# One step's carried state and decay scans, moved ahead of a total and a gated layer on VectorE

## The chip, the cores and the metric

The kernel runs on one core of a Trainium2 chip. A core has five engines, each with its own queue, in which instructions are issued strictly in the order of the program: TensorE (PE in the profile; PEld are its weight loads), VectorE (DVE), ScalarE (ACT), GpSimd (POOL) and SyncE (SP), which here only issues transfers. An engine waits for another one by a semaphore, and whatever stands behind the waiting instruction on its queue waits too. The metric is device time in microseconds, the median of several executions. The profile is of one execution.

## The reference

Two blocks run one behind the other. The first is a state-space scan over 4 batches of 8 heads, 768 tokens long, with heads of 32 columns and a state of 16:

```python
for c in range(nc):                                   # chunks of the sequence
    cum = np.cumsum(la, axis=-1)                      # la = log(clip(a))
    L = np.exp(cum[..., :, None] - cum[..., None, :]) * causal
    M = np.einsum('bhin,bhjn->bhij', Cc, Bc) * L
    y_intra = np.einsum('bhij,bhjd->bhid', M, xc)
    y_inter = np.einsum('bhin,bhnd->bhid', Cc, state) * np.exp(cum)[..., None]
    y[:, :, sl] = y_intra + y_inter
    state = decay_full * state + np.sum(Bx, axis=2)   # carried to the next chunk
```

The second takes the result as 3072 tokens of 256 columns through four experts with 1024 hidden columns each:

```python
for e in range(E):
    h = np.maximum(x @ w1[e], 0.0)
    out += p[:, e:e + 1] * (h @ w2[e])
```

All of it is in float32.

## The kernel before

The scan works in chunks of 128 tokens, 24 in all. Chunks 4k to 4k+3 form block k: one chunk of each of the four batches, at the same place k of the sequence, 512 tokens together. Six blocks follow each other. While the second half of the computation (the experts) works on block k, the scan of block k+1 is done in between.

The experts of a block take eight steps, one for each expert and half of its hidden columns. So n runs over 48 steps, `k, r = divmod(n, 8)`, and r is the step within the block. Steps 0 and 1 are done plainly ahead of the loop; from n = 2 on a step forms its two 2x2 block products from seven products each, with sums in place of the eighth:

- first layer, `fmul(n, 1..7)`: two matmuls each (four records in the profile), gathered in two banks of PSUM called X and Y. `snap` (ScalarE, line 530) copies X aside; `total` (VectorE, line 535) adds a snap to Y; `gated` (VectorE, line 545) applies the maximum with zero and the gate and writes the hidden layer `h`. There are four of these in a step: 11, 22, 21, 12.
- second layer, `smul(n - 1, 1..7)`, one step later: it takes the h's and their four differences T1 to T4 (`diff`, VectorE, line 552), and gathers in four other banks (line 608). T3 and T1 are made at the end of step n, T2 and T4 early in step n+1, from the list `late`.

A bank is written again only when all reads of it are done. Thus `fmul(n, 3)`, which adds into Y, waits for the total of 22, which reads Y as it was before.

Within the steps of block k lies the scan for block k+1, whose chunks are 4k+4 to 4k+7:

- at r = 0, 2, 4, 5 (`scanned`): the decay matrix LT of one chunk, in two halves (VectorE, line 364, `decay_part` 0 and 1), and a small product on GpSimd (line 369);
- at r = 3 and 6 (`scored`), for two chunks together: `masks` (ScalarE), `decay_part(c, 2)`, which is a scan over the decays of one chunk on VectorE (line 347, tile `dec`, from `ah`, which a transfer brings) and a product with it on GpSimd (line 350, tile `cts`); then `scores` (TensorE, line 393, tile `g`), eight matmuls of 32 rows into two banks of their own and into Y and X, and `masked` (VectorE, line 405), the product with LT, eight instructions;
- at r = 4 and 7 (`done`): `outputs` of two chunks (TensorE, lines 450 and 462);
- `carry(c)`, the state that is carried from chunk to chunk (VectorE: a transpose, line 486; for later blocks a multiply-add, line 488; and the masked copy M, line 493). One of these hangs at the end of `late`, behind T2 and T4, in the steps that have one.

The four `scores` of each chunk go to banks `att`, `att`, Y and X. Those on Y wait for the total of 12 and those on X for the gated 21, which free the banks; `masked` waits for all of them.

The order of the work is written out by hand in the loop over n (lines 818 to 919). Nothing is moved by a scheduler. A step that has `scored` issues on VectorE: total and gated 11; the list `late`; total and gated 22; total 12; gated 21; `masked`; gated 12; T3; T1. The variable `behind` is true for r = 3 and r = 6 of block 0, that is n = 3 and n = 6; there the state and the decay scans stand behind gated 21, and in the other blocks they stand ahead of total 12.

GpSimd, in the first eight steps alone, also makes the sums S1 to S4 of the weights (`sum_w1`, `sum_w2`, lines 189 to 193, four instructions for each tile) and stores them to memory for the other blocks (lines 201 and 207). In n = 3 it has the two products of line 350 first, and the sums of w1 of step 5 and w2 of step 4 behind them. SyncE's order of loads in n = 3 is the weights of step 5 and then chunk 7 (tokens and decays).

Of the kernel before, what the change touches and what calls it, by code (L numbers as in the profile page):

```python
# [17 lines left out]
def kernel(  # L18
# [129 lines left out]
    def load_chunk(c):  # L148
        load_tokens(c)
        load_decays(c)  # L150
        load_heads(c)
# [3 lines left out]
    def load_w1(n):  # L155
        e, jj = divmod(n % SPB, JJ)
        t1 = wt1[n] = wts.tile([P, 7, HB], FP32, tag="wt1", name="wt1", bufs=5)
        for k in range(2):
            w = 2 - 2 * k
            a_ = 2 if n < SPB or k else 1  # L160
            nc.sync.dma_start(
                out=t1[:, w:w + a_],
                in_=w1[e, k * P:k * P + P].rearrange("p (a f) -> p a f", a=2)[
                    :, 0:a_, jj * HB:jj * HB + HB])
        if n >= SPB:
            nc.sync.dma_start(out=t1[:, S3:], in_=w1_d[n % SPB])

    def load_w2(n):
        e, jj = divmod(n % SPB, JJ)
        t2 = wt2[n] = wts.tile([P, 7 * HB], FP32, tag="wt2", name="wt2", bufs=5)  # L170
        for i in range(2) if n < SPB else (1,):
            f = i * FH + jj * HB
            nc.sync.dma_start(
                out=t2[:, (1 - i) * 2 * HB:(2 - i) * 2 * HB].rearrange("p (j m) -> p j m", j=JJ),
                in_=w2[e, f:f + HB].rearrange("(j p) m -> p j m", p=P))
        if n >= SPB:
            nc.sync.dma_start(out=t2[:, 2 * HB:], in_=w2_d[n % SPB])
# [137 lines left out]
    def load_gate(k, e):  # L315
        g = gate[k, e] = ffn.tile([P, CPB, P], FP32, tag="gate", name="gate", bufs=3)
        nc.sync.dma_start(out=g, in_=p_d.rearrange(
            "(i k) e s -> k e i s", k=NBLK)[k, e].partition_broadcast(P))
# [54 lines left out]
    def masks(c):  # L373

        s = st[c]
        m = s["ctm"] = att.tile([HN, NT, P], FP32, tag="ctm", name="ctm")
        for t in range(NT):
            nc.scalar.mul(m[:, t], s["xb"][:, OCT:OCT + P], tmask[:, t:t + 1])
# [148 lines left out]
    def snap(n, i):  # L527

        s = first[n][i] = ffn.tile([P, JJ, HB], FP32, tag="snap", name="snap", bufs=4)
        nc.scalar.copy(out=s, in_=first[n]["X"])  # L530

    def total(n, i, b):

        z = first[n]["z" + b] = ffn.tile([P, JJ, HB], FP32, tag="z", name="z", bufs=3)
        nc.vector.tensor_add(z, first[n]["Y"], first[n][i])  # L535

    def gated(n, b, src):

        if n not in hid:
            hid[n] = {}  # L540
        h = hid[n][b] = ffn.tile([P, JJ, HB], FP32, tag="h" + b, name="h" + b)
        k, e = n // SPB, n % SPB // JJ
        half = int(b[1]) - 1
        g = gate[k, e].rearrange("p c s -> p (c s)")[:, half * HB:half * HB + HB]
        nc.vector.scalar_tensor_tensor(  # L545
            out=h, in0=first[n][src], scalar=0.0, in1=g.unsqueeze(1).to_broadcast([P, JJ, HB]),
            op0=ALU.max, op1=ALU.mult)
# [67 lines left out]
    def keep(k, u):  # L615
        e = kept[k, u] = ffn.tile([P, 2, HB], FP32, tag=f"kept{u}", name=f"kept{u}", bufs=1)
        nc.scalar.copy(out=e, in_=acc[k, u])

    def combine(k, part):

        p1, p3 = kept[k, 0][:, 0], kept[k, 0][:, 1]
        if part == 0:
            kept[k, "o"] = ffn.tile([P, 2, BLK], FP32, tag="o", name="o", bufs=1)
            kept[k, "u"] = ffn.tile([P, 3, HB], FP32, tag="u", name="u", bufs=1)
        o, u = kept[k, "o"], kept[k, "u"]
        b1, b2 = slice(0, HB), slice(HB, BLK)
        if part == 0:
            nc.vector.tensor_add(u[:, 0], acc[k, 2][:, 0], p1)
        if part == 1:
            p7, p5 = kept[k, 1][:, 0], kept[k, 1][:, 1]  # L630
            nc.gpsimd.tensor_add(u[:, 1], u[:, 0], p7)
            nc.gpsimd.tensor_add(u[:, 2], u[:, 0], p5)
            nc.gpsimd.tensor_add(o[:, 1, b2], u[:, 1], p5)
            nc.gpsimd.tensor_add(o[:, 0, b2], u[:, 2], p3)
        if part == 2:
            nc.vector.tensor_add(o[:, 0, b1], acc[k, 2][:, 1], p1)
            nc.vector.tensor_add(o[:, 1, b1], acc[k, 3][:, 0], u[:, 1])
            if k == 0 and PLAIN:
                nc.vector.tensor_add(o[:, 1, b2], acc[k, 3][:, 1], o[:, 1, b2])
# [69 lines left out]
    def leave(k, c):  # L709

        for q in range(P // 32):
            for d in range(2):
                leave_part(k, c, q, d, nc.sync)

    def opened(n):

        fmul(n, 1)
        snap(n, 1)
        fmul(n, 2)
# [96 lines left out]
    late = []  # L816
    states = [2, 3]
    for n in range(PLAIN, NS):
        k, r = divmod(n, SPB)

        ahead = CPB * (k + 1)
        scanned = [ahead + d for d in {0: [0], 2: [1], 4: [2], 5: [3]}.get(r, [])]
        scored = [ahead + d for d in {3: [0, 1], 6: [2, 3]}.get(r, [])]
        done = [ahead + d for d in {4: [0, 1], 7: [2, 3]}.get(r, [])]
        if k == NBLK - 1:
            scanned, scored, done = [], [], []
        ending = r == 0 and k > 0
        e = r // JJ
        if r % JJ == 0 and n + JJ < NS:
            load_gate(*divmod(n // JJ + 1, E))  # L830
        if PLAIN + 2 < n + 2 < NS:
            load_w1(n + 2)
            load_w2(n + 2)
        opened(n)
        total(n, 1, "11")
        gated(n, "11", "z11")
        behind = scored and k == 0
        for work in late[:2] if behind else late:
            work()
        if r == 1 and k > 0:  # L840
            combine(k - 1, 0)
            combine(k - 1, 1)
        for c in scanned:
            decay_part(c, 0)
        for c in scored:
            masks(c)
        if k > 0 and 2 <= r < CPB + 2:
            leave(k - 1, r - 2)
        smul(n - 1, 1)
        fmul(n, 6)  # L850
        snap(n, 6)
        smul(n - 1, 3)
        if ending:
            keep(k - 1, 0)
        if done:
            outputs(done)
            states.extend(done)
        fmul(n, 5)
        fmul(n, 7)
        snap(n, 7)  # L860
        total(n, 7, "22")
        smul(n - 1, 7)
        smul(n - 1, 5)
        if ending:
            keep(k - 1, 1)
        gated(n, "22", "z22")
        if r == 1 and k > 0:
            combine(k - 1, 2)
        for c in scanned:
            decay_part(c, 1)  # L870
        for c in scored if not behind else []:
            decay_part(c, 2)
        if n == PLAIN:
            sum_w2(0, 1)
        elif n == SPB - 4:
            sum_w1(n + 2)
        elif n >= SPB - 3:
            sum_w2(n)
        if n < CPB:
            load_chunk(n + CPB)  # L880
        for c in scanned if n >= CPB else []:
            if c + 2 < NCH:
                load_decays(c + 2)
        for c in done:
            if c + CPB < NCH:
                load_tokens(c + CPB)
                load_heads(c + CPB)
        fmul(n, 3)
        total(n, 6, "12")
        fmul(n, 4)  # L890
        gated(n, "21", "X")
        for work in late[2:] if behind else []:
            work()
        for c in scored if behind else []:
            decay_part(c, 2)
        if not scored:
            gated(n, "12", "z12")
        if r == SPB - 1 and k < NBLK - 1:
            sums(k + 1)
        smul(n - 1, 6)  # L900
        if scored:
            scores(scored, ((ps_att, "att"), (ps_att, "att"), (ps_f, "Y"), (ps_f, "X")))
            masked(scored, (3, 2, 0, 1))
            gated(n, "12", "z12")
        smul(n - 1, 2)
        diff(n, "T3", "22", "12")
        smul(n - 1, 4)
        if n == PLAIN:
            sum_w2(1, 1)
        if n != SPB - 4:  # L910
            sum_w1(n + 2)
        if PLAIN < n < SPB - 4:
            sum_w2(n + 1)
        diff(n, "T1", "12", "11")
        if r == 1 and k > 0:
            turned_out(k - 1)
        late = [lambda n=n: diff(n, "T2", "22", "T1"), lambda n=n: diff(n, "T4", "21", "T2")]
        if states:
            late.append(lambda c=states.pop(0): carry(c))
# [48 lines left out]
```

## Time and profile before

| | us |
|---|---|
| median of 4 executions | 639.53 (639.11 to 639.67) |
| the profiled execution | 639.67 |
| its span, first to last instruction | 637.9 |
| TensorE busy | 632.2 (99%) |
| VectorE busy | 485.2 (76%) |
| ScalarE busy | 119.3 (19%) |
| GpSimd busy | 112.7 (18%) |

The granted clock of TensorE is 1.0 throughout. The rows of time that follow give the start in us from the start of the span, the duration, the engine, the line, the operation, its tiles, its shape and the count of instructions that the row merges; in brackets is the idle time of the engine before it, and what ended it. Rows of one engine overlap a little, as an instruction starts before the last one has ended. Step n = 3 lies between about 50.7 us (its first product) and 64.0 us, n = 4 from there to about 79.3 us.

### The profile page before, as it was taken

How to read it: one execution, taken by the hardware profiler on the slowest of the kernel's cores; microseconds unless marked ns; L12 is line 12 of the kernel's file. 1: busy time of each engine (PE TensorE's matmuls, PEld its weight loads, DVE VectorE, ACT ScalarE, POOL GpSimd, SP SyncE). 2: the span in 40 equal slices, each digit the busy share in tenths (PEclk: the TensorE clock that was granted, in tenths of full speed). 3: DMA queues.
4: the chain of work that ended last, by engine and by line, in shares of the span. 5: the costliest groups of instructions: out<-in, count | busy, mean ns of one | idle time of the engine just before them, and what ended most of it. 6: DMA issues, size and time to landing. Idle time of an engine off the chain costs nothing.

```text
span 637.9 us, 9256 instructions
## 1 busy us (share of the span) xinstructions
PE 632.2 (99%) x3405; PEld 536.9 (84%) x3405; DVE 485.2 (76%) x811; ACT 119.3 (19%) x263; POOL 112.7 (18%) x163
## 2 busy tenths in 40 slices
PE   9999999999999999999999999999999999999997
PEld 5888788888888888888888888888888888888886
DVE  7869989788777788678687778778867677756555
ACT  4011121212111221122121211122111211111111
POOL 5786657020001002100002000000100000100001
PEclk9999999999999999999999999999999999999999
DMA  7798893755666392756374576639265744166001
GB/s 221 241 357 297 290 339 159 265 199 166 175 210 243 72 375 72 236 164 237 117 281 162 170 192 197 235 104 357 71 224 163 246 165 133 60 168 226 1 1 33
DMA packets 98512, 121.61 MB, mean 191 GB/s; under 512 B 29528, under 2 KB 81956, under 8 KB 98468
## 3 DMA queue, kind: packets, MB, share of 16 engines
q1 hardware_dynamic: 95512, 111.20, 53.9%
q0 software_dynamic: 2432, 9.50, 3.8%
q8 instruction: 27, 0.44, 0.3%
q10 hardware_dynamic: 524, 0.32, 0.2%
q14 instruction: 17, 0.14, 0.1%
HBM read 108.16 MB, written 12.83 MB: 190 GB/s over the span
## 4 chain that ended last, share of the span: by engine, by line
PE 96%; DVE 2%; issue 1%; POOL 0%; ACT 0%; POOLq 0%; DVEq 0%
PE acc L608 43%; PE X L523 25%; PE Y L523 19%; PE acc L589 2%; PE g L393 2%; PE y L462 2%; PE X L572 1%; PE Y L572 1%; PE y L450 1%; DVE hT L552 1%; DVE MT L405 1%; DVE LT L364 1%; PE t L729 1%; DVE h L545 0%; PE a L331 0%
## 5 line engine op out<-in xcount | busy, mean ns | idle before, releaser
L535 DVE TENSOR_TENSOR z<-Y,snap 128x512 f32<-128x512 f32 x138 | 94.6, 686 | 118.0 <-ACT snap L530 66.7
L608 PE MATMUL acc<-hT,wt 128*128 128x256 f32 x736 | 181.1, 379 | 0.0
L530 ACT COPY snap<-X 128x512 f32<-128x512 f32 x138 | 80.8, 586 | 465.3 <-PE X L523 397.0
L608 PEld LDWEIGHTS acc<-hT,wt 128*128 128x128 f32 x736 | 139.8, 190 | 19.0
L608 PE MATMUL acc<-h,wt 128*128 128x256 f32 x552 | 142.5, 381 | 0.0
L523 PE MATMUL X<-yS,wt 128*128 128x256 f32 x552 | 141.7, 379 | 0.0
L608 PEld LDWEIGHTS acc<-h,wt 128*128 128x128 f32 x552 | 104.0, 190 | 17.0 <-issue 2.7
L523 PEld LDWEIGHTS X<-yS,wt 128*128 128x128 f32 x552 | 104.8, 190 | 14.5 <-issue 0.3
L545 DVE SCALAR_TENSOR_TENSOR h<-z,gate 128x512 f32<-128x512 f32 x138 | 99.8, 723 | 3.5 <-PE acc L589 0.4
L523 PE MATMUL Y<-yT,wt 128*128 128x256 f32 x368 | 94.5, 379 | 1.0 <-DVE z L535 1.0
L523 PEld LDWEIGHTS Y<-yT,wt 128*128 128x128 f32 x368 | 68.7, 190 | 11.9 <-DVE z L535 1.4
L552 DVE TENSOR_TENSOR hT<-h,hT 128x512 f32<-128x512 f32 x92 | 66.1, 719 | 1.8
L552 DVE TENSOR_TENSOR hT<-h,h 128x512 f32<-128x512 f32 x92 | 65.6, 754 | 1.4
L364 DVE TENSOR_TENSOR_SCAN LT<-ab,ident 128x512 f32<-128x512 f32 x42 | 52.1, 1242 | 0.0
L523 PE MATMUL Y<-yS,wt 128*128 128x256 f32 x184 | 48.3, 385 | 0.0
L523 PE MATMUL X<-yT,wt 128*128 128x256 f32 x184 | 47.2, 379 | 0.0
L369 POOL TENSOR_TENSOR MT<-xb,LT 128x128 f32<-128x128 f32 x20 | 8.6, 428 | 205.4 <-PE Y L523 68.8
L405 DVE TENSOR_TENSOR MT<-g,LT 128x256 f32<-128x256 f32 x94 | 32.4, 415 | 10.5 <-PE g L393 10.4
L523 PEld LDWEIGHTS Y<-yS,wt 128*128 128x128 f32 x184 | 34.1, 190 | 6.4 <-issue 2.2
L523 PEld LDWEIGHTS X<-yT,wt 128*128 128x128 f32 x184 | 35.0, 190 | 4.8
L545 DVE SCALAR_TENSOR_TENSOR h<-X,gate 128x512 f32<-128x512 f32 x50 | 34.2, 684 | 5.2 <-PE X L523 3.6
L350 POOL TENSOR_TENSOR cts<-ctm,dec 128x256 f32<-128x256 f32 x20 | 14.1, 726 | 130.1 <-DVE dec L347 130.1
(103 smaller groups left out, 324.4 us busy)
## 6 DMA issues: line engine op xcount, KB each, us to landing
wt<-in_w_dram SPq DMA_DIRECT2D x112, 256.0 KB
wt<-w_d SPq DMA_DIRECT2D x40, 640.0 KB
wt<-w_d SPq DMA_DIRECT2D x40, 512.0 KB
ab<-acut_d SPq DMA_DIRECT2D x21, 512.0 KB
gate<-p_d SPq DMA_DIRECT2D x23, 256.0 KB
w_d<-wt POOLq DMA_DIRECT2D x8, 640.0 KB, 5.1
wt<-in_w_dram SPq DMA_DIRECT2D x40, 128.0 KB
w_d<-wt POOLq DMA_DIRECT2D x8, 512.0 KB, 7.3
```

The costliest lines, as they stand in the source:

```text
L350: nc.gpsimd.tensor_mul(cts, s["ctm"], dec.unsqueeze(1).to_broadcast([HN, NT, P]))
L364: nc.vector.tensor_tensor_scan(out=LT[:, i * w:i * w + w], data0=s["a"][i], data1=ident.rearrange("p h s -> p (h s)")[:, :w], initial=0.0, ...
L393: nc.tensor.matmul(out=g.rearrange("p t s -> p (t s)"), lhsT=s["xb"][k, OBT:OBT + P], rhs=s["ctm"][k].rearrange("p t s -> p (t s)"), start ...
L405: nc.vector.tensor_mul(s["MT"][:, h, 0:P], s["g"][q], s["LT"][:, h])
L462: nc.tensor.matmul(out=y[32 * q:32 * q + 32, t, 0:w], lhsT=s["xb"][:, h * D:h * D + D], rhs=s["MT"][:, NT * q + t, 0:w], start=(k == 0 and ...
L523: nc.tensor.matmul(out=f[bank][:, j], lhsT=wt1[n][:, w, j * P:j * P + P], rhs=rhs, start=(i in (1, 2, 5) and j == 0), stop=(j == JJ - 1), ...
L530: nc.scalar.copy(out=s, in_=first[n]["X"])
L535: nc.vector.tensor_add(z, first[n]["Y"], first[n][i])
L545: nc.vector.scalar_tensor_tensor(out=h, in0=first[n][src], scalar=0.0, in1=g.unsqueeze(1).to_broadcast([P, JJ, HB]), op0=ALU.max, op1=ALU. ...
L552: nc.vector.tensor_sub(h[o], h[x], h[y])
L572: nc.tensor.matmul(out=f[bank][:, j], lhsT=wt1[n][:, w, j * P:j * P + P], rhs=yT[k][:, i, cols], start=(i == 0 and j == 0), stop=(i == 1), ...
L608: nc.tensor.matmul(out=acc[k, u][:, half], lhsT=w2_op(n, w)[:, j], rhs=rhs[:, j], start=(begins and j == 0), stop=(n % SPB == SPB - 1 and ...
```

## The change

At r = 3 of block 0 (n = 3) the carried state (transpose and M) and the two decay scans are issued behind the gated 22 instead of behind the gated 21, so that total 12 and gated 21 follow them. At r = 6 of block 0 (n = 6) their place stays as it was. All other blocks keep theirs. The GpSimd products that belong to the scans keep their place in GpSimd's queue.

```diff
@@ -835,6 +835,7 @@
         total(n, 1, "11")
         gated(n, "11", "z11")
         behind = scored and k == 0
+        last = behind and r == 6
         for work in late[:2] if behind else late:
             work()
         if r == 1 and k > 0:
@@ -868,7 +869,9 @@
             combine(k - 1, 2)
         for c in scanned:
             decay_part(c, 1)
-        for c in scored if not behind else []:
+        for work in late[2:] if behind and not last else []:
+            work()
+        for c in scored if not last else []:
             decay_part(c, 2)
         if n == PLAIN:
             sum_w2(0, 1)
@@ -889,9 +892,9 @@
         total(n, 6, "12")
         fmul(n, 4)
         gated(n, "21", "X")
-        for work in late[2:] if behind else []:
+        for work in late[2:] if last else []:
             work()
-        for c in scored if behind else []:
+        for c in scored if last else []:
             decay_part(c, 2)
         if not scored:
             gated(n, "12", "z12")
```

## The prediction

> **What bounds the kernel now.** I read the page first, then the list of what TensorE (PE) waited for, then the time rows of each engine around the change. On the page:
>
> ```profile
> PE   9999999999999999999999999999999999999997
> PEclk9999999999999999999999999999999999999999
> ...
> PE 96%; DVE 2%; issue 1%; POOL 0%; ACT 0%; POOLq 0%; DVEq 0%
> ```
>
> TensorE is busy in every slice at full granted clock, and the chain that ended last is 96% TensorE. A change on VectorE (DVE) is therefore worth only what it alters of TensorE's few waits. These are all of them over 0.05 us:
>
> ```profile
> PE Y L523 <- DVE z L535: 1.0, 1, 1.0
> PE t L729 <- PEq L960: 0.8, 1, 0.8
> PE y L428 <- POOL MT L369: 0.5, 1, 0.5
> PE turned L655 <- DVE o L686: 0.3, 1, 0.3
> ```
>
> Three lie in the opening or at the very end, where the diff touches nothing. The first is the kernel's one wait in its main loop, and it lies in step n=4, one step behind the edit (r=3 of sequence block 0 is n=3):
>
> ```profile
> 71.98 1.89 PE L608 MATMUL acc<-hT,wt 128*128 128x256 f32 x8
> 74.86 1.13 PE L523 MATMUL Y<-yT,wt 128*128 128x256 f32 x4 [0.98 <-DVE z L535]
> ```
>
> Product 3 of the first layer writes into the bank that the total on VectorE (line 535) still reads. Four matmul records take 0.86 us from start to start (the rows of n=3 start at 58.44, 59.30, 60.17). So eight from 71.98 let the next begin at 73.71. It began at 74.86, 1.15 late, and its four took 1.13 where four in full stride take 1.03, another 0.10. The wait costs **1.25 us in all**, and that is the ceiling of any gain here.
>
> Why the total is late shows in VectorE's rows. From 62.34 to 74.80 it has no idle time to speak of:
>
> ```profile
> 58.26 0.69 DVE L545 SCALAR_TENSOR_TENSOR h<-z,gate 128x512 f32<-128x512 f32 x1
> 59.50 0.69 DVE L535 TENSOR_TENSOR z<-Y,snap 128x512 f32<-128x512 f32 x1 [0.56 <-PE Y L523]
> 60.37 0.69 DVE L545 SCALAR_TENSOR_TENSOR h<-X,gate 128x512 f32<-128x512 f32 x1 [0.17 <-PE X L523]
> 60.98 0.20 DVE L486 STREAM_TRANSPOSE S<-A 128x32 f32<-128x32 f32 x1
> 61.21 0.29 DVE L493 TENSOR_TENSOR M<-S,qmask 128x128 f32<-128x128 f32 x1
> 61.42 0.73 DVE L347 TENSOR_TENSOR_SCAN dec<-ah,zeros 128x128 f32<-128x128 f32 x2
> 62.34 2.74 DVE L405 TENSOR_TENSOR MT<-g,LT 128x256 f32<-128x256 f32 x8 [0.18 <-PE g L393]
> 65.00 1.25 DVE L545 SCALAR_TENSOR_TENSOR h<-z,gate 128x512 f32<-128x512 f32 x1
> 66.28 2.76 DVE L552 TENSOR_TENSOR hT<-h,h 128x512 f32<-128x512 f32 x2
> 68.96 0.68 DVE L535 TENSOR_TENSOR z<-Y,snap 128x512 f32<-128x512 f32 x1
> 69.68 0.69 DVE L545 SCALAR_TENSOR_TENSOR h<-z,gate 128x512 f32<-128x512 f32 x1
> 70.28 2.35 DVE L552 TENSOR_TENSOR hT<-h,hT 128x512 f32<-128x512 f32 x2
> ```
>
> The product with the mask (line 405) waited 0.18 us for TensorE's scores, so what stands ahead of it is not what makes the chain late. Behind it three groups are long: 1.25 for a gated layer that takes 0.69 elsewhere, and 2.76 and 2.35 for two differences that take 1.41 where GpSimd (POOL) stands still (the pair at 82.61). GpSimd works all that time, because it started late:
>
> ```profile
> 61.99 1.41 POOL L350 TENSOR_TENSOR cts<-ctm,dec 128x256 f32<-128x256 f32 x2 [3.42 <-DVE dec L347]
> ```
>
> It idled 3.42 us for the first decay scan, and its eight weight sums and two stores queue behind that.
>
> **The change part by part.** The instruction orders of the two kernels differ on VectorE alone, in n=3: transpose, M and two decay scans go from behind total 12 and gated 21 to ahead of them. Step r=6 keeps its order, and so do later blocks. No count changes. TensorE, ScalarE, GpSimd, SyncE and all DMA issues keep their order; no step passes another on SP's or POOL's queue.
>
> *(a) The four move into VectorE's idle time, and a little over.* From S at 60.98 to the next free start they take 0.44 (to 61.42) plus the scans' 0.65 (in block 1 the scans start at 163.18 and the next total at 163.83): 1.09. The idle time there is 0.56 before total 12 and 0.17 before gated 21. New order: gated 22 at 58.26, S 0.61 later at 58.87 (as 60.37 to 60.98), total 12 at 59.96 instead of 59.50, gated 21 at 60.54 (0.58 later, as from 76.58 to 77.16), ending at 61.23 instead of 61.06. Queued behind it are TensorE's scores, which take bank X from it. In n=6 of this trace gated 21 ended at 101.11 + 0.68 = 101.79 and the scores began at 101.82, so they follow by about 0.05 with their fourth matmul, the one on X. In n=3 they began at 61.12, the one on X 0.02 later; it would now start near 61.28. **Loss: 0.15 us**, between 0 (block 1, with the scans but no transpose or M ahead, loses nothing) and 0.46 (the whole delay of total 12). I take 0.15, as block 1 gives nearly the same: 0.44 more work against 0.27 that gated 21 idles there (164.68 less 163.83 and 0.58).
>
> The first scan would now start at 59.31, 2.11 earlier, and needs its decays from a DMA; they were issued before 34 us, and at 61.42 nothing waited for them. That wait costs nothing unless they landed after 59.31.
>
> *(b) GpSimd starts 2.1 us earlier.* Its two products would run from 59.89 to 61.3, and the weight sums of two tiles behind them. Nothing else holds these: their loads were issued by 46 us. Four sums at 0.73 with gaps of 0.08 end at 64.3: they lie beside VectorE's work on PSUM, where rows of both engines keep their length (62.3 to 64.7). The first store would be issued from 64.6 to 65.2 and the last four sums begin at 65.2 instead of 67.75.
>
> *(c) VectorE's chain behind the scores.* The mask product starts at 62.34 + 0.15 = 62.49 and its last eighth frees VectorE at 65.15. There it meets the store and the next sum. The dearest row of this meeting is gated 22 at 98.95: 1.64 us, with the store 98.70 to 99.27 and a sum to 100.03. Then the pattern at 77.76 to 80.71 repeats (gated, then two differences, against four sums): 2.23 for the pair. So gated 12 ends near 66.5 (66.25 before), the differences end near 68.8 (69.04), total 11 runs to 69.4, gated 11 to 70.1. Here the sums end too: four from 65.2 at 0.74, 1.07, 1.06, 1.17 with gaps of 0.08 end near 69.4, where they ended at 72.09. The second pair of differences finds GpSimd idle: 1.41 instead of 2.35. It ends near 71.4 (72.63). Transpose, M and scan bring total 22 of n=4 to 72.9, but then ScalarE's snap is late next: it ended at 72.18 + 0.58 = 72.76, now 72.91. The total starts at 73.0 and ends near 73.7; TensorE would come to it at 73.71 + 0.15 = 73.86. **The wait goes: -1.25 us**, by a margin of about 0.15.
>
> [...]
>
> *(d) Afterwards.* GpSimd's next product waits for VectorE's scan of n=4, so both engines fall back into step with TensorE, about 1.1 us earlier, and n=6 finds the phases it had. I cost this at nothing; the cover is that TensorE waits for no transfer anywhere in the trace. If the phase in n=6 did slip, gated 21 there has no slack at all, and each 0.1 us costs 0.1.
>
> Sum: -1.25 + 0.15 = **-1.10 us**. The profiled execution took 639.67 (span 637.9 and 1.8 around it), so its like would take 638.57. It stands 0.14 above the median of four, 639.53; against the median I predict **638.4**, 0.17% less. A change under 0.2% (1.28 us) is about what a measurement of this kernel cannot tell from none, and the ceiling of 1.25 lies just under it.
>
> **The rivals.**
> - *The chain is shortened only in part.* VectorE loses one more turn to a sum than I count (0.55 us, what a difference at 1.21 to 1.25 has over 0.69), perhaps two. The margin of 0.15 takes the first of it, and TensorE waits 0.4 to 0.95 and the 0.10 of a restart: -0.6 to 0, 638.9 to 639.6. For it: a difference at 67.31 took 1.73. Against it: only four sums are left where six were.
> - *The whole ceiling.* The score on X hides its 0.15 behind the three scores ahead of it, and the wait goes: -1.25, 638.3; with the scatter of the runs (0.56 between the four) this can show as faster than 0.2%. For it: four scores start within 0.02 and run side by side. Against: the next four are queued behind them in order.
> - *Nothing is gained.* GpSimd's sums do not start earlier, because a weight load or an old store holds them. Then VectorE meets the same sums, its chain is late by the 0.15 of the scores as well: +0.15, 639.7. Against it: at 63.37 the first sum followed the products without a gap, on loads issued 17 us before.
> - *Slower: the decays land late.* The two scans stand now ahead of gated 21, so if a transfer of chunk 5's decays lands after 59.65, gated 21, the scores and TensorE wait for it, us for us. The trace has no landing time for them; they had landed by 61.75, when the scan ran. At most that is 61.75 - 59.65 = 2.1 us, and 0.15 of (a): +2.25, 641.8, if nothing of the old wait is saved. It decides from a landing after 59.65 + 1.13 = 60.8. Against it: they were issued near 33 us, and where landings are shown (the stores) the medians are 5.1 and 7.3 us.
>
> **How the numbers follow.** Forecast 0.60, partly 0.15, ceiling 0.12, nothing gained 0.08, late decays or something else that costs TensorE 0.05. Forecast and ceiling with the scatter of the medians reach past -1.28 in about a quarter of cases: faster 0.24. Slower by 1.28 takes late decays, or a phase slip in n=6 beyond what I see: 0.06. The same: 0.70. The range goes from 637.9 (the ceiling and half of the scatter, 0.3 to 0.4) to 639.7 (nothing gained), which leaves out about 0.1 on each side.
>
> **What would show it.** Right: TensorE's list of waits without the one for the total on line 535; the scores of n=3 at 61.12 with their last starts 0.1 to 0.2 later; the two products of line 350 near 59.9; the last sum's end near 69.4; the second pair of differences at 1.41; all after it about 1.1 earlier. Wrong in (a): a wait of TensorE before the scores of over 0.3. Wrong in (b): products at 59.9 and a gap before the first sum. Wrong in (c): differences of over 2.3 for the second pair, and a wait before product 3 of n=4. Wrong in (d): a wait of TensorE in n=6 or for a weight.

## The result

The changed kernel takes 638.52 us (median of 34 executions, 637.82 to 638.55) against 639.56 us before (54 executions, 638.91 to 639.67): 1.04 us less, a ratio of 0.9983 with a 95% interval of 0.9978 to 0.9988. That is 0.17% faster. The prediction was 638.4.

The page of the profile after, span 636.3 us, execution 638.08 us; the chain that ended last, then the whole list of what TensorE waited for, then TensorE's scores of n=3 and product 3 of n=4:

```profile
PE 98%; DVE 1%; issue 0%; POOL 0%; ACT 0%; POOLq 0%
```

```profile
PE t L729 <- PEq L963: 0.8, 1, 0.8
PE y L428 <- POOL MT L369: 0.5, 1, 0.5
PE turned L655 <- DVE o L686: 0.3, 1, 0.3
```

```profile
60.67 1.29 PE L393 MATMUL g<-ctm,xb 32*128 32x256 f32 x16
...
73.40 1.03 PE L523 MATMUL Y<-yT,wt 128*128 128x256 f32 x4
```

The wait for the total on line 535 is gone, and nothing has come in its place; product 3 runs in full stride (1.03). The scores stretched a little; before the change their row was:

```profile
61.12 1.15 PE L393 MATMUL g<-ctm,xb 32*128 32x256 f32 x16
```

VectorE's rows of n=3 and n=4 after (start, duration, engine, line, operation, tiles, shape, count, idle time before):

```profile
57.81 0.69 DVE L545 SCALAR_TENSOR_TENSOR h<-z,gate 128x512 f32<-128x512 f32 x1
58.41 0.21 DVE L486 STREAM_TRANSPOSE S<-A 128x32 f32<-128x32 f32 x1
58.66 0.29 DVE L493 TENSOR_TENSOR M<-S,qmask 128x128 f32<-128x128 f32 x1
58.86 0.73 DVE L347 TENSOR_TENSOR_SCAN dec<-ah,zeros 128x128 f32<-128x128 f32 x2
59.51 0.67 DVE L535 TENSOR_TENSOR z<-Y,snap 128x512 f32<-128x512 f32 x1
60.10 0.68 DVE L545 SCALAR_TENSOR_TENSOR h<-X,gate 128x512 f32<-128x512 f32 x1
62.00 2.74 DVE L405 TENSOR_TENSOR MT<-g,LT 128x256 f32<-128x256 f32 x8 [1.22 <-PE g L393]
64.66 1.38 DVE L545 SCALAR_TENSOR_TENSOR h<-z,gate 128x512 f32<-128x512 f32 x1
66.07 2.23 DVE L552 TENSOR_TENSOR hT<-h,h 128x512 f32<-128x512 f32 x2
...
69.55 1.41 DVE L552 TENSOR_TENSOR hT<-h,hT 128x512 f32<-128x512 f32 x2
...
72.49 0.69 DVE L535 TENSOR_TENSOR z<-Y,snap 128x512 f32<-128x512 f32 x1
```

All starts here are 0.45 us earlier than in the profile before, already ahead of the edit (gated 22: 57.81 and 58.26), so 0.45 is to be added when the two are compared. The second pair of differences takes 1.41 instead of 2.35, the first 2.23 instead of 2.76, while gated 12 takes 1.38 instead of 1.25. The idle time ahead of the mask product has grown from 0.18 to 1.22: VectorE's early work bought idle time there, not an earlier mask product. What did change is GpSimd:

```profile
59.44 1.41 POOL L350 TENSOR_TENSOR cts<-ctm,dec 128x256 f32<-128x256 f32 x2 [1.32 <-DVE dec L347]
...
64.12 0.59 POOL L201 DMA_DIRECT2D w_d<-wt  x1 [0.30 <-POOL wt L193]
64.74 0.74 POOL L189 TENSOR_TENSOR wt<-wt 128x256 f32<-128x256 f32 x1
...
67.72 1.18 POOL L193 TENSOR_TENSOR wt<-wt 128x256 f32<-128x256 f32 x1
```

It idled 1.32 us instead of 3.42, and its last sum ends at 68.90 (69.35 with the 0.45 added) instead of 72.09, where the row of before ends:

```profile
70.92 1.17 POOL L193 TENSOR_TENSOR wt<-wt 128x256 f32<-128x256 f32 x1
```

Set instruction against instruction, TensorE's starts in the two traces differ by three steps and by nothing else up to the last matmul: -0.45 left from the opening, +0.14 at the scores of n=3, -1.25 at product 3 of n=4. The first is not the change's. It goes with the clock: the trace's record of a full granted clock begins 6.4 us after the start of the span in the profile before and 4.2 us in the one after, and the matmuls of the opening run slow until then. (So "1.0 throughout", said of the profile before, holds from 6.4 us on.) The first row is of before, the second of after:

```profile
4.03 1.24 PE L331 MATMUL a<-a_q,const-float32-1.0 32*128 32x256 f32 x8
```

```profile
4.04 0.77 PE L331 MATMUL a<-a_q,const-float32-1.0 32*128 32x256 f32 x8
```

The profiles of the experiments below bear this out. In the six of the nine in which the record begins at 5.4 us or later, three of them of kernels built from the changed one, TensorE's starts agree from 7.5 us on until the scores of n=3; in the three that begin at 4.2, 3.9 and 3.7 they are 0.45, 0.58 and 0.67 ahead. This scatter is in every set of executions of either kernel (639.67 and 638.91 before, 638.55 and 637.82 after), so the change is worth -1.25 + 0.14 = -1.11 us by the trace, -1.04 by the medians and -1.12 between the slowest execution of each.

### The profile page after: what moved, and what is told of

Same layout as the page of the kernel before. It is cut to its first block, busy times and chain, and to the rows that moved or that the text cites. A ratio compares the mean times of both kernels' runs of the same rounds, so it can differ in the third digit from the quotient of the medians.

```text
span 636.3 us, 9256 instructions
## 1 busy us (share of the span) xinstructions
PE 631.6 (99%) x3405; PEld 537.1 (84%) x3405; DVE 483.7 (76%) x811; ACT 119.3 (19%) x263; POOL 112.1 (18%) x163
## 4 chain that ended last, share of the span: by engine, by line
PE 98%; DVE 1%; issue 0%; POOL 0%; ACT 0%; POOLq 0%
PE acc L608 44%; PE X L523 25%; PE Y L523 19%; PE acc L589 2%; PE y L462 2%; PE g L393 2%; PE X L572 1%; PE Y L572 1%; PE y L450 1%; PE t L729 1%; DVE LT L364 0%; PE a L331 0%; PE y L428 0%; DVE MT L405 0%; PE turned L655 0%
## 5 line engine op out<-in xcount | busy, mean ns | idle before, releaser
L552 DVE TENSOR_TENSOR hT<-h,hT 128x512 f32<-128x512 f32 x92 | 65.2, 709 | 1.8
```

Of the source, the lines that this page charges most:

```text
L552: nc.vector.tensor_sub(h[o], h[x], h[y])
```

## The experiments

Theory A, the prediction's: the gain comes from GpSimd, which starts 2.1 us earlier and so no longer works against VectorE when the chain behind the scores is late; the price is paid at the scores. Theory B: the gain comes from VectorE's four instructions, which are no longer in that chain.

**Only the scans ahead (e1).** From the kernel before:

```diff
-        for c in scored if not behind else []:
+        for c in scored if not behind or r == 3 else []:
             decay_part(c, 2)
...
-        for c in scored if behind else []:
+        for c in scored if behind and r != 3 else []:
             decay_part(c, 2)
```

> Only the two decay scans of n=3 go ahead of total 12; the transpose and M stay behind gated 21. Theory A (the gain is GpSimd's early start, which leaves VectorE's chain behind the scores uncontended): scans at 58.87 on the clock of the profile before, products of line 350 near 59.45, the wait for line 535 in n=4 gone (-1.25), and gated 21 no later than before, so the scores of n=3 keep their full stride and the 0.14 that the change loses there is saved too: 638.4 against 638.5 of the change, seen in the trace rather than in the time. Theory B (VectorE's four instructions themselves were taken out of the late chain): only the scans' 0.65 of the 1.09 is taken out, so about 0.6 of the wait is gone and 0.4 stays: 638.9.

Measured: 638.40 us, ratio 0.9982 (0.9973 to 0.9991). VectorE's and TensorE's rows:

```profile
60.37 0.69 DVE L545 SCALAR_TENSOR_TENSOR h<-X,gate 128x512 f32<-128x512 f32 x1 [0.17 <-PE X L523]
60.98 0.20 DVE L486 STREAM_TRANSPOSE S<-A 128x32 f32<-128x32 f32 x1
61.21 0.48 DVE L493 TENSOR_TENSOR M<-S,qmask 128x128 f32<-128x128 f32 x1
62.34 2.74 DVE L405 TENSOR_TENSOR MT<-g,LT 128x256 f32<-128x256 f32 x8 [0.65 <-PE g L393]
```

```profile
61.12 1.15 PE L393 MATMUL g<-ctm,xb 32*128 32x256 f32 x16
...
73.71 1.03 PE L523 MATMUL Y<-yT,wt 128*128 128x256 f32 x4
```

From 7.5 us on the starts of this profile agree with those of before, so they can be compared as they stand. Gated 21 and the scores are where they were, and product 3 begins at 73.71 instead of 74.86, in full stride: the whole ceiling of 1.25, with no loss at the scores. The transpose and M stood in the idle time ahead of the mask product all along, at no cost. Theory B's 638.9 is excluded, as the whole wait is gone although the mask product began at 62.34 in both. No other version that was run does better. Its lead of 0.14 over the change is seen in the trace alone; the times (638.40 and 638.52) point the same way, but their intervals overlap.

**GpSimd's sums first, VectorE as before (e2).** From the kernel before:

```diff
         gated(n, "21", "X")
+        if n == 3:
+            sum_w1(n + 2)
         for work in late[2:] if behind else []:
...
-        if n != SPB - 4:
+        if n not in (3, SPB - 4):
             sum_w1(n + 2)
```

> VectorE, TensorE and ScalarE keep the order of the kernel before; GpSimd alone makes the four sums of w1 of step 5 and their store ahead of the two products of line 350, in the 3.42 us that it idled. Theory A: the sums run from 58.6 and the last four begin near 64 instead of 67.75, the second pair of differences takes 1.41 and the wait in n=4 goes: -1.25 with no loss at the scores, 638.3; up to 0.4 less, 638.7, if M and the scans, which read SBUF twice, now meet the sums and let the mask product begin late. Theory B: VectorE's order is as before, so nothing is gained: 639.5.

Measured: 638.42 us, ratio 0.9983 (0.9974 to 0.9992). VectorE issues in the order of before, and yet the wait is gone:

```profile
57.68 1.68 DVE L545 SCALAR_TENSOR_TENSOR h<-z,gate 128x512 f32<-128x512 f32 x1
...
60.71 0.88 DVE L493 TENSOR_TENSOR M<-S,qmask 128x128 f32<-128x128 f32 x1
...
62.16 2.71 DVE L405 TENSOR_TENSOR MT<-g,LT 128x256 f32<-128x256 f32 x8
...
69.31 1.41 DVE L552 TENSOR_TENSOR hT<-h,hT 128x512 f32<-128x512 f32 x2
```

Starts in this profile are 0.58 earlier than in the one before, from the opening. The collisions moved to gated 22 (1.68) and M (0.88), and the mask product has no idle time before it any more; it even began 0.40 later than before (62.16 and 0.58 against 62.34). TensorE lost 0.05 at the scores and gained the 1.25. Theory B, which gives 639.5, falls: the order on VectorE is not what the gain comes from.

**The change with GpSimd held back (e3).** Three spare additions on GpSimd, from the changed kernel:

```diff
         for c in scored if not last else []:
             decay_part(c, 2)
+        if n == 3:
+            for _ in range(3):
+                spare = att.tile([P, 2 * P], FP32, tag="spare", name="spare", bufs=3)
+                nc.gpsimd.tensor_add(spare, ident[:, 0:2].rearrange("p h s -> p (h s)"), ident[:, 2:4].rearrange("p h s -> p (h s)"))
```

> The changed kernel with three spare additions of 128x256 on GpSimd between the products of line 350 and the sums, about 2.1 us, which lie beside VectorE's mask product; VectorE's order is that of the change. Theory A: the sums begin again about where they did in the kernel before (near 63.2), the gated 12 and both pairs of differences are long again (some 2.7 and 2.3 for the pairs), and TensorE waits 0.8 to 1.1 in n=4, with the 0.14 at the scores on top: 639.4 to 639.7. Theory B: VectorE's work is as early as in the change, so the time stays at 638.5.

Measured: 639.59 us, ratio 1.0 (0.9991 to 1.0009): the whole gain is taken back. GpSimd, VectorE and TensorE:

```profile
61.27 2.09 POOL L879 TENSOR_TENSOR spare<-ident 128x256 f32<-128x256 f32 x3
63.32 0.71 POOL L189 TENSOR_TENSOR wt<-wt 128x256 f32<-128x256 f32 x1
```

```profile
66.24 2.76 DVE L552 TENSOR_TENSOR hT<-h,h 128x512 f32<-128x512 f32 x2
...
70.25 2.35 DVE L552 TENSOR_TENSOR hT<-h,hT 128x512 f32<-128x512 f32 x2
```

```profile
74.81 1.13 PE L523 MATMUL Y<-yT,wt 128*128 128x256 f32 x4 [0.80 <-DVE z L535]
```

With VectorE's order that of the change and the sums back at 63.32 (63.37 before), the differences take 2.76 and 2.35 again, to the hundredth, and the wait is back. So theory A is shown from both sides: moving GpSimd alone gives the gain, holding GpSimd alone takes it.

**Step r=6 treated like r=3 (e4).** In the changed kernel, `last = False`.

> The changed kernel with r=6 (n=6) treated like r=3: transpose, multiply-add, M and two scans ahead of total 12 there too. In the profile before, gated 21 of n=6 ended at 101.79 with no idle time of VectorE ahead of it and the scores began at 101.82. Theory A, part (d): no slack there, so the scores and TensorE are late by the whole block, 101.71 to 103.61, 1.9 us, and nothing is won behind them, as VectorE idles 1.57 before the next total that TensorE could wait for: 640.4. Theory B: work that goes ahead of the scores is work out of the chain, and costs nothing or gains: 638.5 or less.

Measured: 638.94 us, ratio 0.9989 (0.9981 to 0.9998): 0.42 slower than the change, where I expected 1.9. VectorE in n=6:

```profile
97.84 0.69 DVE L545 SCALAR_TENSOR_TENSOR h<-z,gate 128x512 f32<-128x512 f32 x1
98.45 0.20 DVE L486 STREAM_TRANSPOSE S<-A 128x32 f32<-128x32 f32 x1
...
99.18 0.73 DVE L347 TENSOR_TENSOR_SCAN dec<-ah,zeros 128x128 f32<-128x128 f32 x2
99.83 0.67 DVE L535 TENSOR_TENSOR z<-Y,snap 128x512 f32<-128x512 f32 x1
```

Gated 22 takes 0.69 where it took 1.64, and the block (from the transpose to total 12) 1.38 instead of 1.9. I had overlooked a queue: in n=6 a weight tile's sums stand between the two places in the program, so the products of line 350, which go with the scans, were moved ahead of these sums on GpSimd's queue. GpSimd waited for the scans, and behind a store that ended at 98.16 it was quiet while gated 22 and the block ran. The block's 1.38 less the 0.95 that gated 22 saved is 0.43, the loss at the scores.

**The same with GpSimd's order kept (e5).** The scan and the product of `decay_part(c, 2)` are split; in n=6 the state and the scans (part 3) go ahead, the products (part 4) stay. From the changed kernel, without the lines that make the two parts:

```diff
-        for work in late[2:] if behind and not last else []:
+        for work in late[2:] if behind else []:
             work()
-        for c in scored if not last else []:
-            decay_part(c, 2)
+        for c in scored:
+            decay_part(c, 3 if last else 2)
...
-        for work in late[2:] if last else []:
-            work()
         for c in scored if last else []:
-            decay_part(c, 2)
+            decay_part(c, 4)
```

> The kernel of the run with both steps ahead, with one difference: in n=6 the two GpSimd products of line 350 stay behind gated 21 in the program, so that GpSimd keeps the order of the kernel before (a weight tile's four sums and store, then the products) while VectorE has transpose, multiply-add, M and scans ahead of total 12. Theory A now: the loss in n=6 was only 0.42 because the products went ahead of the sums on GpSimd's queue and gated 22 lost its collision (0.69 instead of 1.64); with GpSimd's order restored gated 22 takes 1.64 again, gated 21 and the scores of n=6 are late by the block of 1.4 to 1.9, and TensorE loses that: 639.9 to 640.4. Rival C: there is a slack at the scores of n=6 that the trace does not show, and the loss stays near 0.42: 638.9.

Measured: 642.82 us, ratio 1.006 (1.0047 to 1.0074). Rival C falls, but my own number was too small by 2.4. VectorE, then TensorE, then windows of 2 us with busy time and count of PE, PEld, DVE, ACT and POOL, granted clock, DMA share and GB/s:

```profile
97.84 1.65 DVE L547 SCALAR_TENSOR_TENSOR h<-z,gate 128x512 f32<-128x512 f32 x1
...
100.36 1.75 DVE L347 TENSOR_TENSOR_SCAN dec<-ah,zeros 128x128 f32<-128x128 f32 x2
102.03 0.66 DVE L537 TENSOR_TENSOR z<-Y,snap 128x512 f32<-128x512 f32 x1
```

```profile
102.74 1.72 PE L395 MATMUL g<-ctm,xb 32*128 32x256 f32 x12 [1.34 <-DVE z L537]
104.40 2.07 PE L610 MATMUL acc<-h,wt 128*128 128x256 f32 x4
```

```profile
102.00:104.00 2.00, 1.26 (x11) 0.91 (x12) 1.29 (x3) 0.00 (x0) 1.85 (x3) 1.00 0.39 161
104.00:106.00 2.00, 2.00 (x10) 1.40 (x6) 1.50 (x5) 0.00 (x0) 1.84 (x4) 0.60 0.41 166
106.00:108.00 2.00, 2.00 (x7) 1.61 (x6) 1.97 (x6) 0.00 (x0) 1.70 (x3) 0.55 0.00 0
```

Two things add up. Gated 22 collides again (1.65) and the two scans as well (1.75 instead of 0.73): gated 21, and with it the last score, is 2.6 late. And behind the scores the matmuls run at half speed, four in 2.07 instead of 1.13, at a granted clock of 0.60 and 0.55 in these windows; the trace's clock record is at 0.5 from 104.39 to 107.81. Set instruction against instruction with the changed kernel, TensorE falls back 2.6 us up to the last score and 1.7 more while the clock is low, which is half of those 3.4 us: 4.3 in all.

**The price of a delay, by itself (e6, e7).** In the kernel of e1, two (e6) or four (e7) spare transposes on VectorE behind the scans of n=3; the edit of e6:

```diff
             decay_part(c, 2)
+        for _ in range(2 if n == 3 else 0):
+            spare = att.tile([P, NQ * P], FP32, tag="spare", name="spare", bufs=1)
+            nc.vector.transpose(spare, ident.rearrange("p h s -> p (h s)"))
```

> The kernel with the two scans alone ahead, and two spare transposes of 128x512 on VectorE behind them in n=3 (about 0.65 to 0.7 each, one input, so that they do not meet GpSimd). By theory A the slack ahead of gated 21 is 0.27 and nothing else covers a delay: gated 21, the scores and TensorE are about 1.05 late, total 22 of n=4 still comes in time as it waits for ScalarE's snap, and the time is 638.4 + 1.05 = 639.4, the granted clock staying at 1.0 as it did over the wait of 0.98 in the kernel before. A rival to the slack (the scores wait elsewhere, and only part of a delay of gated 21 reaches TensorE) gives under 638.9.

> The same with four spare transposes: 2.7 us ahead of total 12, gated 21 and the scores about 2.4 late. If the delay alone counts, 638.4 + 2.4 = 640.8. If a pause of this length also halves TensorE's clock for 3.4 us, as it did in n=6 of the run with VectorE's block ahead and GpSimd's order kept (granted clock 0.60 and 0.55 in two windows of 2 us there), some 1.7 to 1.9 come on top: 642.5 to 642.7, with a granted clock well under 1 behind the scores of n=3. If that run's loss had been something of n=6 alone, the clock stays at 1.0 here.

Measured: e6 639.37 us (0.9999, 0.999 to 1.0009), 0.97 above the median of e1; six of ten executions lie between 639.33 and 639.44, and the clock is 1.0. The profile, which starts 0.68 earlier from the opening, has:

```profile
60.77 0.68 DVE L545 SCALAR_TENSOR_TENSOR h<-X,gate 128x512 f32<-128x512 f32 x1
```

```profile
60.45 2.18 PE L393 MATMUL g<-ctm,xb 32*128 32x256 f32 x16
```

The transposes put total 12 off by 1.35, gated 21 by 1.08 (60.77 and 0.68 against 60.37 in e1), and TensorE behind the scores by 1.03. So what exceeds the slack of 0.27 reaches TensorE nearly whole. The two spare transposes took 1.43 us, and the four of e7 2.92, with GpSimd at work beside them (1.92 of the 2 us from 60.00 in e7): 0.7 each, as expected. The transpose of line 486, which has one input as well, takes 0.20 in the profile before both beside a sum (101.71) and where GpSimd stands still (83.94). e7: median 640.79 us (1.004, 1.0022 to 1.0058), but in three groups: six executions at 640.20 to 640.79, which is the delay of 2.4 alone, one at 642.54 and three at 644.23 to 644.25. The mean granted clock of the executions divides them in the same way: 1.0 in the six, 0.997 in the one, 0.995 in the three. The profile is of one at 644.23:

```profile
63.07 2.40 PE L393 MATMUL g<-ctm,xb 32*128 32x256 f32 x12 [1.24 <-DVE z L535]
65.39 2.07 PE L608 MATMUL acc<-h,wt 128*128 128x256 f32 x4
```

```profile
62.00:64.00 2.00, 0.93 (x8) 0.62 (x11) 1.97 (x5) 0.00 (x0) 1.74 (x3) 0.99 0.77 282
64.00:66.00 2.00, 2.00 (x12) 1.16 (x5) 0.55 (x3) 0.00 (x0) 1.79 (x3) 0.50 0.61 155
```

Here the granted clock fell to one half from 63.98 to 70.81 us, 6.83 us, and TensorE lost 3.4 us on top of the 2.4. So the halved clock is not a matter of n=6. It follows the pause in some executions of the same kernel and not in others; at a delay of 1.03 (e6) and over the wait of 0.98 in the kernel before, no trace shows it.

## Why the prediction was right, and where it was not

*(a) The block and the scores.* Predicted 0.15, measured 0.14. With the 0.45 added, total 12 started at 59.96 (59.96 predicted) and gated 21 at 60.55 (60.54). The rival of the whole ceiling, in which the three scores ahead hide this, falls, but not for the reason that was given against it: the next four are not all held up. In each of the four rounds of four scores three begin on time and one begins 0.14 late (60.83, 61.15, 61.37 and 61.59 in the trace after), and the product that follows begins behind the last of these. e1 and e6 confirm the slack that the number rests on: the scans alone fit into it, and with two transposes more gated 21 is late by what exceeds it.

*(b) GpSimd.* Its products were predicted at 59.89 and began there; the store at 64.6, measured 64.57; the last four sums from 65.2 to 69.4, measured 65.19 to 69.35. "Nothing is gained", where an old load or store holds the sums, did not happen.

*(c) The chain.* Gated 12 was predicted to end near 66.5 and ended at 66.49; the pairs took 2.23 and 1.41 as predicted; total 22 started at 72.94 (73.0). The snap it also needs ended at 72.46 in the trace after, 0.03 before it started at 72.49, as predicted; VectorE's own work ahead of it ended at 72.54, so the two arrived together. The total ended at 73.18 and TensorE began product 3 at 73.40, at full stride: 0.22, of which the hand-over takes some 0.05 (74.81 to 74.86 before), against the margin of 0.15. e2 and e3 show that it is GpSimd's time that decides. The rival of a chain shortened in part came this near: one more turn lost to a sum, which it priced at 0.55, would have been more than the margin.

*(d) Afterwards.* Right for the change: the two traces differ by a constant from n=4 to the end, and n=6 found its old phases. Two statements in it and in the rivals did not hold in general. "Each 0.1 us costs 0.1" in n=6 holds for the 0.42 of e4, but not for every delay, as e5 shows there and e7 in n=3: with a delay of 2.6 in e5 and of 2.4 in the profile of e7, the clock added 1.7 and 3.4 us, and with the 1.03 of e6 nothing. The rival of the late decays, priced at +2.25 us for 2.1 of delay, may therefore be priced too low at its far end; a delay of 2.1 was not run. And when I wrote the expectation of e4, I left out GpSimd's queue, which is the very thing that (b) rests on.

The size: -1.10 predicted, -1.11 by the trace, -1.04 between the medians. The gap between the last two is the scatter of the opening, which differs from one execution to the next by up to 0.7 us.

## What to carry to other kernels

Where one engine is the bound, list its waits first: they are the ceiling of what a reordering elsewhere can bring, here 1.25 us of 639. Then ask what the late engine was slowed by, and not only what it had to do. Here the cure was to let a third engine start its side work in a stretch where neither engine slows the other (four sums at 0.72 to 0.73 each beside the scores and the mask product), and the same gain came from moving that engine's work alone; a step that feeds another queue moves that queue as well, and its instructions are counted there too.

## What the runs showed of the hardware that was not expected

- A pause of TensorE can cost more than its length. With the last scores 2.6 and 2.4 us late, the granted clock fell to 0.5 for 3.41 us in the profile of e5 and for 6.83 us, twice that, in the one of e7, and matmul records came every 0.43 us instead of 0.22, which cost 1.7 and 3.4 us on top of the delay. TensorE's whole idle stretch was 1.34 us in e5 and 1.24 in e7, between matmuls of 32 rows; over the 0.98 in the kernel before, the clock held at 1.0. Six executions of e7 took 640.20 to 640.79 at a mean clock of 1.0. What makes the clock fall in one execution and not in another was not shown, as these six left no trace.
- A gated layer that reads two tiles in SBUF (the memory that holds all tiles but those in PSUM) took longer than its 0.69 where VectorE started it during a weight store that a sum follows: 1.38 after, 1.64 in n=6 before, 1.65 in e5, 1.68 in e2, each ending 0.5 to 0.6 after the sum, which had started later than VectorE's own instruction. With no sum behind the store it took its 0.69 (82.00 beside the store at 81.60 before), and with a product of line 369 behind the store 0.78 (49.29 before). In e1 gated 12 started at 65.00, 0.25 after the sum, and took 1.05. What in the store or the sum makes it so was not tried.
- The decay scans were also longer beside GpSimd's sums: two took 1.75 in e5, at 100.36, beside the sums that started at 100.15 and 100.99, and 0.73 in the other rows shown.
